# Attention and a gated feed-forward layer on one core: the last pair of token blocks in 26 products of 2x4x4 pieces in place of 28

## The chip, the cores and the metric

The kernel runs on one core of one Trainium2 chip. The metric is device time in microseconds (us) for one execution. Five engines work side by side: TensorE (PE in the profile; its weight loads are PEld), VectorE (DVE), ScalarE (ACT), GpSimd (POOL) and SyncE (SP), which issues the transfers. Each engine takes its own instructions in order and meets the others only through semaphores.

## The reference, cut to what matters

```python
scores = where(masks, q @ k.T / sqrt(64), -1e9)          # 8 batches x 8 heads, 576 x 576
attn   = softmax(scores) @ v
x      = attn.transpose(0, 2, 1, 3).reshape(4608, 512)
gate   = 1 / (1 + exp(-(x @ w_gate)))                     # w_gate, w_val: 512 x 1536
out    = (gate * (x @ w_val)) @ w_out                     # w_out: 1536 x 512
```

Heads 0 to 3 see a local window of 32 keys, heads 4 to 7 see keys at the same position modulo 32. All data is float32.

## The kernel before, in words

The tokens are cut into 9 blocks of 512. Blocks 0, 1 and 2 are multiplied plainly. The other six are taken two at a time: the constant `SUPER = (3, 5, 7)` names the first block of each pair, and the attention of later batches runs between the products of earlier blocks. Every float32 product is made of three TensorE instructions of 128 x 512: the high half of the weights times the high half of x, high times low, low times high. Each high half is a cast on ScalarE, each low half a subtraction (whole minus high) on VectorE or GpSimd.

For a pair k, gates and values are computed for two slices of 128 output features at a time (index q, six of them). One such unit multiplies two token blocks by two halves of the 512 input features by two feature slices, and Strassen's way takes 7 products in place of 8 (steps G for gates and V for values, `half_product`, L986). Each product covers two chunks of 128 input features, so it has 2 x 3 = 6 TensorE instructions: 7 x 6 x 2 x 6 = 504 for a pair. Results are summed in two PSUM banks for the gate and two for the value (tiles p and d). ScalarE copies some banks out (`keep_sum`, step c, L1008), VectorE adds the others to those copies (`add_sum`, step ad, L1013), ScalarE takes the sigmoid (sg) and VectorE multiplies gate and value (`gate_times`, step mu, L1030 and L1027). The 30 products of gate and value stay in SBUF as tiles `hid`.

The output of a pair is made in 7 products again (steps O, Oa, Ob, `out_half`, L1065, 252 TensorE instructions). Their operands are differences of `hid` tiles (`out_sum`, steps ta to td, L1036), split into a high half on ScalarE (hx, L1050) and a low half (hy on VectorE, hyp on GpSimd, L1054). There is room for five such operands at a time. While the output of one pair runs, the x operands of the next pair are made: differences of raw x (`diff`, xd on GpSimd, xdv on VectorE, L960), high halves (xh, L968) and low halves (xl, xlp, L972).

The weights in their sums and halves lie in DRAM (`sets`, `osets`) and come back through a ring of six places of 512 KB (`load_group`, steps r, L938 and L942), issued by SP.

The order of all this is one long list of step names, `ORDER`, written by a planner outside the program. The program walks the list once; each engine gets its instructions in the order of the list.

Of the kernel before, what the change touches and what calls it, by code (L numbers as in the profile page):

```python
# [22 lines left out]
P = 128  # L23
# [47 lines left out]

BANKS = {
# [18 lines left out]
fN0.3 wlp2.0 fg0.0.0 fP0.2 fX0.2 fW0.3 wb0.1 wa0.1 fg1.0.0 fH0.2 ws0.1 wr3.0 wb1.1 fT0.3 fL0.2 wa1.1 wd0.1 fR0.2 wr3.2 ws1.1 fg0.0.1 fP0.3 wd1.1 fS1.0
wu0.1 wu1.1 wl0.1 wb0.2 wlp1.1 fg1.0.1 fM1.0 fQ1.1 wa0.2 fg0.1.0 fA1.0 wr4.0 fg0.0.2 wa2.1 fU1.0 fg0.1.1 wb2.1 ws2.1 fX0.3 fE1.0 fY1.0 wr4.2 ws0.2
wdp2.1 wb1.2 fn1.0 fg1.1.0 fH0.3 fN1.0 wu2.1 fg0.1.2 fL0.3 fWp1.0 wa1.2 fg1.1.1 fR0.3 ws1.2 wr5.0 fg1.0.2 wlp2.1 fB1.0.1 fg0.0.3 fg0.1.3 fB1.0.0 s0.0
wdp0.2 fg1.0.3 wb2.2 m0.0 wa2.2 fg1.1.2 wdp1.2 fB1.0.2 x0.0 wr5.1 fg2.0.0 s0.1 fg2.1.0 y0.0 wu0.2 fg2.0.1 wu1.2 fB1.0.3 wa3.0 fg2.0.2 wb3.0 wb3.2
wl0.2 fg1.1.3 wl1.2 wa3.2 wa4.1 fg2.1.1 fg2.1.2 wa3.1 fg2.0.3 ws2.2 m0.1 fX1.0 wdp2.2 ws3.0 fZ1.1 fS1.1 ws4.1 ws3.2 ws3.1 wd3.0 fH1.0 fR1.0 fL1.0
fg2.1.3 wb3.1 wr6.0 wa4.0 x0.1 wu3.0 wdp3.1 wu3.1 wb4.0 wr6.2 y0.1 s0.2 m0.2 x0.2 wu2.2 wr5.2 ws4.0 wd4.0 wu4.0 wl4.0 wb5.0 o0.0 wdp3.2 o0.1 wu3.2
# [131 lines left out]
def attention_then_glu(ctx, tc, qk_l, qk_s, v_l, v_s, w_all, consts, out, out_t):  # L228
# [433 lines left out]
    def bank(tag, name):  # L662
        return (ps_a if tag == "a" else ps).tile([P, 2 * BANK], F32, tag=tag, name=name)
# [260 lines left out]
    for k in SUPER:  # L924
        units += [(k, q, p) for q in range(PAIRS) for p in USE] + [(k, p, u) for p in USE_OUT for u in range(PAIRS // 2)]
# [305 lines left out]
```

## Time and profile before

| What | Value |
|---|---|
| Three runs | 899.38, 900.62 and 901.22 us; median 900.62 us |
| Profiled execution, first to last instruction | 897.2 us |
| TensorE busy | 889.0 us, 99% of the span, 7050 matmuls |
| VectorE, ScalarE, GpSimd busy | 628.8, 477.8 and 327.8 us |
| Transfers | 193.63 MB, 216 GB/s over the span |
| Granted TensorE clock | 1.000 of full speed |

The profiled execution has no time of its own but its span of 897.2 us, which begins at the first and ends at the last instruction; the median of the three runs is 3.4 us above it, for what lies around the instructions and from run to run. A busy share is the time in which an engine has an instruction under way, waits inside an instruction included.

### The profile page before, as it was taken

To read this page: it belongs to the slowest core of one execution; us is meant where nothing else is said; L and a number is where in the kernel's file an instruction comes from. 1 tells how busy PE (TensorE), PEld (TensorE's weight loads), DVE (VectorE), ACT (ScalarE), POOL (GpSimd) and SP (SyncE) were. 2 spreads that over 40 slices of the span, in tenths; PEclk is the share of its full clock that TensorE was granted. 3 is DMA by queue.
4 is the path that set the end of the run, shared out by engine and by line. 5 is a ranking of instruction groups with operands and counts; after the bars stand their busy time and mean duration, and the time that the engine had idled before them with its cause. 6 is when DMAs were issued, how large, how long until landed. Compare 5 with 4: busy or idle time off the path is not lost.

```text
span 897.2 us, 17941 instructions
## 1 busy us (share of the span) xinstructions
PE 889.0 (99%) x7050; PEld 726.1 (81%) x7050; DVE 628.8 (70%) x1025; ACT 477.8 (53%) x869; POOL 327.8 (37%) x392
## 2 busy tenths in 40 slices
PE   8999999999999999999999999999999999999998
PEld 5788888888887788888878888888888888888886
DVE  6888877677778887889998976556667723433553
ACT  5888765443445554576564654344455623423453
POOL 4452631434663544675633420100132300221362
PEclk9999999999999999999999999999999999999999
DMA  9864685553573667898878758666655667655664
GB/s 349 331 229 138 217 280 168 165 163 109 158 247 99 178 182 267 245 323 288 252 249 274 258 181 271 219 205 198 216 180 194 214 192 232 195 176 204 235 205 148
DMA packets 116869, 193.63 MB, mean 216 GB/s; under 512 B 7600, under 2 KB 58800, under 8 KB 116784
## 3 DMA queue, kind: packets, MB, share of 16 engines
q1 hardware_dynamic: 116784, 192.47, 65.3%
q8 instruction: 56, 0.92, 0.4%
q14 instruction: 29, 0.24, 0.1%
HBM read 149.98 MB, written 42.47 MB: 214 GB/s over the span
## 4 chain that ended last, share of the span: by engine, by line
PE 89%; DVE 7%; ACT 2%; DMA 1%; issue 1%; SPq 0%; DVEq 0%; ACTq 0%
PE p L986 21%; PE oc L1065 19%; PE d L986 15%; PE o L713 10%; PE g L682 9%; PE v L682 9%; PE s L425 1%; PE x L603 1%; DVE pt L537 1%; PE gv L682 1%; PE x L575 1%; PE s_g L425 1%; DMA qk<-in_qk_l 1%; DVE sb L474 1%; ACT sb L489 1%
## 5 line engine op out<-in xcount | busy, mean ns | idle before, releaser
L986 PE MATMUL p<-xs,ring 128*128 128x512 f32 x864 | 210.9, 391 | 0.1
L986 PEld LDWEIGHTS p<-xs,ring 128*128 128x128 f32 x864 | 161.3, 188 | 34.2 <-issue 0.5
L986 PE MATMUL d<-xs,ring 128*128 128x512 f32 x648 | 160.0, 390 | 0.2 <-DVE hid L1013 0.2
L986 PEld LDWEIGHTS d<-xs,ring 128*128 128x128 f32 x648 | 121.2, 188 | 26.4 <-DVE hid L1013 0.9
L1065 PE MATMUL oc<-hh,ring 128*128 128x512 f32 x312 | 103.8, 389 | 0.0
L713 PE MATMUL o<-w,hh 128*128 128x512 f32 x288 | 90.5, 395 | 0.0
L1013 DVE TENSOR_TENSOR e<-e,d 128x512 f32<-128x512 f32 x54 | 37.0, 684 | 72.6 <-PE d L986 55.6
L682 PE MATMUL g<-xh,w 128*128 128x512 f32 x256 | 85.8, 393 | 0.8 <-DVE sb L449 0.5
L682 PE MATMUL v<-xh,w 128*128 128x512 f32 x256 | 85.0, 390 | 0.0
L1036 POOL TENSOR_TENSOR hid<-hid,hid 128x512 f32<-128x512 f32 x23 | 31.0, 1351 | 113.5 <-DVE hid L1030 87.8
L1065 PE MATMUL oc<-ops,ring 128*128 128x512 f32 x288 | 72.3, 389 | 0.0
L1050 ACT CAST hh<-hid 128x512 fp32r<-128x512 f32 x78 | 46.7, 620 | 42.9 <-PE oc L1065 31.5
L1065 PEld LDWEIGHTS oc<-hh,ring 128*128 128x128 f32 x312 | 58.6, 188 | 12.2
L1008 ACT COPY e<-p 128x512 f32<-128x512 f32 x54 | 31.7, 587 | 66.9 <-PE p L986 57.1
L1013 DVE TENSOR_TENSOR hid<-hid,d 128x512 f32<-128x512 f32 x54 | 36.8, 681 | 39.5 <-PE d L986 21.9
L898 POOL TENSOR_TENSOR sum<-w 128x256 f32<-128x256 f32 x49 | 39.4, 823 | 67.3 <-DMA sets<-sum 43.6
L1065 PEld LDWEIGHTS oc<-ops,ring 128*128 128x128 f32 x288 | 54.0, 188 | 11.3
L713 PEld LDWEIGHTS o<-w,hh 128*128 128x128 f32 x288 | 53.0, 188 | 11.4
L1008 ACT COPY hid<-p 128x512 f32<-128x512 f32 x54 | 31.7, 588 | 54.5 <-PE p L986 54.3
L1065 PE MATMUL oc<-hl,ring 128*128 128x512 f32 x156 | 60.7, 389 | 0.0
L903 POOL TENSOR_TENSOR sum<-sum 128x128 f32<-128x128 f32 x100 | 53.3, 534 | 18.8 <-DVE sum L898 5.5
L537 DVE STREAM_TRANSPOSE pt<-sb 32x320 f32<-32x320 f32 (+1 forms) x112 | 55.4, 495 | 3.3 <-POOL pt L376 1.0
(178 smaller groups left out, 1717.8 us busy)
## 6 DMA issues: line engine op xcount, KB each, us to landing
ring<-sets SPq DMA_DIRECT2D x126, 512.0 KB, 4.9
ring<-osets SPq DMA_DIRECT2D x63, 512.0 KB, 4.5
raw<-in_w_all SPq DMA_DIRECT2D x36, 512.0 KB, 5.7
qk<-in_qk_l SPq DMA_DIRECT2D x14, 608.0 KB, 5.0
qk<-in_qk_s SPq DMA_DIRECT2D x14, 594.0 KB, 5.4
sets<-w SPq DMA_DIRECT2D x24, 256.0 KB, 4.6
sets<-sumh SPq DMA_DIRECT2D x24, 256.0 KB, 2.9
sets<-sum SPq DMA_DIRECT2D x24, 256.0 KB, 3.1
```

The costliest lines, as they stand in the source:

```text
L425: nc.tensor.matmul(sc[j % len(sc)][g * m : (g + 1) * m, j // len(sc) * BANK + (s - lo) * kk : j // len(sc) * BANK + (s - lo + 1) * kk], q[ ...
L537: nc.vector.transpose(dst[band * LB : (band + 1) * LB, at : at + n, col * LB : (col + 1) * LB], src[part * LB : (part + 1) * LB, x : x + n ...
L682: nc.tensor.matmul(o, w, x, start=first and n == 0, stop=last and n == len(todo) - 1)
L713: nc.tensor.matmul(acc[k][i], h[:, i * P : (i + 1) * P], w, start=f == 0 and n == 0, stop=f == NF - 1 and n == 2,)
L898: by.tensor_tensor(to, part(wh[f][i], c), part(wl[f][i], c), op=ALU.add)
L903: by.tensor_tensor(u[:, to], u[:, x], u[:, y], op=op)
L986: nc.tensor.matmul(to, w[:, (wi * 2 + c) * P : (wi * 2 + c + 1) * P], x[xi][:, c], start=p in (1, 2, 5) and c == j == 0, stop=c == 1 and j ...
L1008: nc.scalar.copy(x, two[m, 0])
L1013: nc.vector.tensor_tensor(x, x, two[m, 1], op=ALU.add)
L1036: by.tensor_tensor(h[to], h[x], h[y], op=ALU.subtract)
L1050: nc.scalar.copy(ops[q, p][0], hidden_tile(k, q, KEPT[str(p)]))
L1065: nc.tensor.matmul(chains[m, at], w[:, (wi * 2 + m) * P : (wi * 2 + m + 1) * P], x[xi], start=p in (1, 2, 5) and q == j == 0, stop=q == PA ...
```

## The change

The gates and values of the last pair (blocks 7 and 8) are multiplied in another way. The unit is now two token blocks by four chunks of input features by four feature slices (index n, three of them, in place of six q). A scheme of 26 products replaces four times 7 = 28. Each product covers one chunk of 128 input features and so has 3 TensorE instructions: 26 x 3 x 2 x 3 = 468 for the pair in place of 504. The output of the pair is computed as before.

- The weight side has 24 sums per unit for the gate and 24 for the value (`W_SUMS`, 33 steps bu for each of the six combinations of n and gate or value, 128 x 128 each, 32 on GpSimd and one on ScalarE), then six high halves (bh, ScalarE) and six low halves (bw, VectorE), stored to DRAM by 14 transfers (bd) into `quad`, where four products lie side by side in rows of 2 KB. Two more slices are stored raw by `plain_sets`. The words that the sums start from are stored in DRAM while the earlier pairs' sets are made (wq, 24 transfers of 256 KB) and read back (bl, 6 transfers of 1 MB).
- The x side has 18 sums (`X_SUMS`, 12 on GpSimd as xq, 6 on VectorE as xqv), 24 high halves (xu, ScalarE) and 24 low halves (12 xw on VectorE, 12 xwp on GpSimd), in places listed in `SPOTS` and `X_AT`.
- The PSUM banks: the eight banks are eight tiles, four for the gate (m = 0) and four for the value (m = 1). A product p adds into the bank `CHAIN[p]`; running sums are read between products. `TAKEN` lists the 26 reads per gate or value: 8 copies on ScalarE (c) and 18 sums on VectorE (+, -, r). A bank is used again four products of the same kind later, with four of the other kind between. Gates end in tiles `ga`, then sigmoid (gs) and product (gm, 24 in all).
- The planner wrote the whole of `ORDER` anew. TensorE's own order is the same as before up to the first product of the last pair.

```diff
+PRODUCTS = 26
+CHAIN = (0, 1, 2, 3, 0, 1, 2, 3, 0, 1, 2, 3, 0, 1, 2, 3, 0, 1, 2, 3, 0, 1, 2, 3, 2, 3)
+CHAIN_STARTS = (0, 1, 2, 3, 18, 19)
+TAKEN = """
+0c1 1c5 2c6 3c0 4+5 5+1 6+0 6c3 7+6 7c7 8-7 9+3 12+3 13-7 14+1 15-5 16c2 17c4 18-0 19-6 20-6 21+0 22r2 23+4 24r3 25-7
+"""
...
+        if k == LAST:
+            units += [(k, "quad", n) for n in range(QUADS * PRODUCTS // 2)]
+        else:
+            units += [(k, q, p) for q in range(PAIRS) for p in USE]
...
+    def x_sum(n, by=nc.gpsimd):
+        to, a, b, op = x_sums[n]
+        by.tensor_tensor(x_word(to), x_word(a), x_word(b), op=ALU.add if op == "+" else ALU.subtract)
...
+    def x_low(n, by=nc.vector):
+        by.tensor_tensor(x_spot(X_AT[n][1]), x_word(f"x{n}"), x_spot(X_AT[n][0]).bitcast(F32), op=ALU.subtract)
...
+    def store_quad(n, m, u):
+        w = quad[n, m]
+        for part, x in ((0, word_high_at(w, u).bitcast(F32)), (1, w[u])):
+            for p, at, size in ((4 * u, 0, 4),) if u < 5 else ((20, 0, 2), (24, 2, 2)):
+                to = place_of(m, p)
+                nc.sync.dma_start(quad_set(n)[:, to // 4, part, to % 4 : to % 4 + size], x[:, at : at + size])
...
+    def quad_product(n, m, p):
+        at = place_of(m, p)
+        w = ring[LAST, "quad", n * (PRODUCTS // 2) + at // 4][:, :, at % 4]
+        x = X_OF[p]
+        high, low = (x_spot(n) for n in X_AT[x][:2])
+        for j, (wi, xi) in enumerate(((0, high), (0, low), (1, high))):
+            nc.tensor.matmul(
+                quad_bank(m, CHAIN[p]), w[:, wi], xi, start=p in CHAIN_STARTS and j == 0, stop=j == 2, skip_group_check=True
+            )
...
+    def take(n, m, j):
+        p, o, op = taken[j]
+        x, to = quad_bank(m, CHAIN[p]), part_of(n, m, o)
+        if op == "c":
+            nc.scalar.copy(to, x)
+        elif op == "r":
+            nc.vector.tensor_tensor(to, x, to, op=ALU.subtract)
+        else:
+            nc.vector.tensor_tensor(to, to, x, op=ALU.add if op == "+" else ALU.subtract)
```

What the new list does to the engines is seen in two places. The first is GpSimd while the output of the pair 5 is multiplied and just behind it. Before, the end of that stretch is this; `hl` and `ops` are low halves of output operands, `xs` low halves of x for the pair 7, `hid` sums for outputs. The last three rows already belong to the products of the pair 7.

```order
L1054 TENSOR_TENSOR ops_7207<-hid_9_7266,ops_7207 128x512
L1054 TENSOR_TENSOR ops_7207<-hid_11_7402,ops_7207 128x512
L1054 TENSOR_TENSOR hl_1_4_8090<-hid_3_6835,hh_1_4_8089 128x512
L1036 TENSOR_TENSOR hid_8_7222<-hid_8_7222,hid_7_7170 128x512
L1054 TENSOR_TENSOR ops_7207<-hid_8_7222,ops_7207 128x512
L1054 TENSOR_TENSOR hl_5_4_8125<-hid_13_7584,hh_5_4_8124 128x512
L972 TENSOR_TENSOR xs_3_1_7702<-xraw_7669,xs_3_0_7675 128x512
L1036 TENSOR_TENSOR hid_4_8395<-hid_3_8369,hid_2_8303 128x512
L1054 TENSOR_TENSOR hl_1_1_8425<-hid_2_8303,hh_1_1_8424 128x512
L1036 TENSOR_TENSOR hid_2_8303<-hid_4_8395 128x512
```

Now the same place reads as follows; L1163 is a sum of x pieces, L1169 a low half of x for the pair 7, L1292 a low half of an output operand of the pair 5.

```order
L1163 TENSOR_TENSOR xs_9_8340<-xraw_7845,xs_7_8004 128x512
L1163 TENSOR_TENSOR xs_12_8045<-xraw_7845,xs_10_8016 128x512
L1163 TENSOR_TENSOR xs_h_8348<-xraw_7845,xs_12_8045 128x512
L1163 TENSOR_TENSOR xs_9_8340<-xraw_7163,xs_7_8004 128x512
L1292 TENSOR_TENSOR ops_7974<-hid_9_7492,ops_7974 128x512
L1169 TENSOR_TENSOR xs_3_8111<-xs_7_8004,xs_2_8326 128x512
L1292 TENSOR_TENSOR ops_7974<-hid_11_7680,ops_7974 128x512
L1292 TENSOR_TENSOR hl_1_4_8420<-hid_3_7000,hh_1_4_8419 128x512
L1292 TENSOR_TENSOR ops_7974<-hid_8_7442,ops_7974 128x512
L1169 TENSOR_TENSOR xs_1_8188<-xs_6_7965,xs_0_7919 128x512
L1292 TENSOR_TENSOR hl_5_4_8481<-hid_13_7897,hh_5_4_8480 128x512
L1169 TENSOR_TENSOR xs_5_8400<-xs_8_8184,xs_4_8209 128x512
```

The same output operands are there, and between them now stand sums and low halves of x, most of which VectorE made before or which are new. From the first to the last TensorE instruction of this output, the list gives GpSimd 27 instructions of 128 x 512 (14 before), and VectorE 48 whose two inputs both lie in SBUF (55 before) and 8 that read a PSUM bank (6 before).

The second place is VectorE among the products of the last pair. Before, a stretch of it reads as follows; the rows with a tile `d` or `p` read a PSUM bank, the others multiply gate and value.

```order
L1013 TENSOR_TENSOR e_3_1_8580<-e_3_1_8580,d_3_8571 128x512
L1013 TENSOR_TENSOR hid_7_8588<-hid_7_8588,d_3_8615 128x512
L1030 TENSOR_TENSOR hid_7_8588<-hid_7_8588,e_3_1_8580 128x512
L1013 TENSOR_TENSOR hid_9_8656<-hid_9_8656,d_3_8615 128x512
L1013 TENSOR_TENSOR e_3_7_8646<-e_3_7_8646,d_3_8571 128x512
```

Now such a stretch, in the second of the three groups, is this; `q_2`, `q_3`, `qa`, `qg` and `qv` are PSUM banks, `qu` and `qw` weight sums (L1207 is a low half of them), L1268 multiplies gate and value.

```order
L1260 TENSOR_TENSOR ga_6_8900<-ga_6_8900,qg 128x512
L1207 TENSOR_TENSOR qu_0_8880<-qu_0_8880,qw_1_8878 128x512
L1258 TENSOR_TENSOR ga_2_9070<-q_2_8507,ga_2_9070 128x512
L1207 TENSOR_TENSOR qu_2_8884<-qu_2_8884,qw_1_8878 128x512
L1260 TENSOR_TENSOR hid_8_8973<-hid_8_8973,qv 128x512
L1260 TENSOR_TENSOR ga_4_9077<-ga_4_9077,q_3_8508 128x512
L1258 TENSOR_TENSOR hid_7_9093<-q_2_8511,hid_7_9093 128x512
L1260 TENSOR_TENSOR hid_6_8939<-hid_6_8939,q_3_8512 128x512
L1207 TENSOR_TENSOR qu_1_8887<-qu_1_8887,qw_1_8878 128x512
L1260 TENSOR_TENSOR ga_0_8928<-ga_0_8928,qa_8506 128x512
```

Low halves of the weights for the third group stand among the reads of the banks that the second group's products fill. From the first product of the last pair to the first of its output, the list gives VectorE 150 instructions: 107 that read a bank and 43 with both inputs in SBUF. Before they were some 61, 42 of them reads of a bank.

## Rows read from the trace of the kernel before

**Rows 1.** The page: busy time, and the granted clock in 40 slices.

```profile
PE 889.0 (99%) x7050; PEld 726.1 (81%) x7050; DVE 628.8 (70%) x1025; ACT 477.8 (53%) x869; POOL 327.8 (37%) x392
...
PEclk9999999999999999999999999999999999999999
```

**Rows 2.** Stretches: start:end, length, busy us (instructions) per engine, clock, DMA share, GB/s.

```profile
543.50:664.95 121.45, 121.45 (x850) 100.17 (x850) 70.50 (x114) 58.94 (x108) 16.23 (x19) 1.00 0.65 211
664.95:722.07 57.12, 57.12 (x253) 47.31 (x253) 42.18 (x62) 31.95 (x57) 18.29 (x13) 1.00 0.62 206
722.07:836.31 114.24, 114.24 (x505) 94.62 (x505) 40.53 (x60) 37.73 (x66) 16.31 (x13) 1.00 0.61 201
836.31:893.46 57.15, 57.14 (x252) 46.92 (x251) 30.32 (x38) 25.86 (x45) 28.98 (x22) 1.00 0.57 194
893.46:897.20 3.74, 0.00 (x0) 0.00 (x0) 0.00 (x0) 0.59 (x1) 0.00 (x0) 1.00 0.37 140
```

**Rows 3.** The chain that ended last, in order of time: start us, us, what.

```profile
664.95 57.12 PE oc L1065 x252
...
836.31 57.15 PE oc L1065 x252
```

**Rows 4.** Waits of VectorE from 722 to 840 us: total us, times, longest.

```profile
DVE e L1013 <- PE d L986: 32.8, 13, 7.5
```

**Rows 5.** Timeline of VectorE, 664 to 700 us: start us, us, instruction.

```profile
670.24 1.69 DVE L1036 TENSOR_TENSOR hid<-hid 128x512 f32<-128x512 f32 x1
671.84 0.68 DVE L960 TENSOR_TENSOR xd<-xraw,xd 128x512 f32<-128x512 f32 x1
672.45 0.68 DVE L1054 TENSOR_TENSOR hl<-hid,hh 128x512 fp32r<-128x512 f32 x1
673.05 0.68 DVE L1036 TENSOR_TENSOR hid<-hid 128x512 f32<-128x512 f32 x1
```

**Rows 6.** Timeline of GpSimd, 664 to 723 us.

```profile
670.08 1.29 POOL L1054 TENSOR_TENSOR hl<-hid,hh 128x512 fp32r<-128x512 f32 x1 [2.46 <-ACT hh L1050]
```

**Rows 7.** Timeline of GpSimd, 493 to 512 us.

```profile
495.54 1.75 POOL L960 TENSOR_TENSOR xd<-xraw,xd 128x512 f32<-128x512 f32 x1
497.25 1.73 POOL L1036 TENSOR_TENSOR hid<-hid 128x512 f32<-128x512 f32 x1
```

**Rows 8.** Timeline of VectorE in the same stretch.

```profile
496.49 1.35 DVE L1054 TENSOR_TENSOR hl<-hid,hh 128x512 fp32r<-128x512 f32 x1 [0.35 <-ACT hh L1050]
497.76 1.77 DVE L1054 TENSOR_TENSOR ops<-hid,ops 128x512 fp32r<-128x512 f32 x1
```

**Rows 9.** Groups of instructions from 500 us on: xcount, busy us, mean ns, idle before.

```profile
L1013 DVE TENSOR_TENSOR e<-e,d 128x512 f32<-128x512 f32 x36 | 24.7, 687 | 67.0 <-PE d L986 52.6 <-ACT e L1008 14.3
L1008 ACT COPY hid<-p 128x512 f32<-128x512 f32 x36 | 21.2, 588 | 47.8 <-PE p L986 47.7
```

**Rows 10.** GpSimd's sums of 128 x 128, whole execution, the same columns.

```profile
L903 POOL TENSOR_TENSOR sum<-sum 128x128 f32<-128x128 f32 x100 | 53.3, 534 | 18.8 <-DVE sum L898 5.5 <-ACT hid L1008 3.4 <-issue 2.9
```

**Rows 11.** Transfers from 722 to 836 us: total, and issues with median us to landing.

```profile
DMA packets 11377, 22.93 MB, mean 201 GB/s; under 512 B 721, under 2 KB 721, under 8 KB 11371
...
ring<-sets SPq DMA_DIRECT2D x38, 512.0 KB, 4.6
```

More of the change, by code (lines that the diff above doesn't have):

```diff
@@ L91 @@
[L91 to L94, printed above, removed]
@@ L876, in plain_sets @@
                 nc.sync.dma_start(sets[q][:, 7 * i + 2, n], b[:, 1])
+            for p in W_RAW:
+                k, f = divmod(W_RAW[p], 4)
+                if f // 2 == q % 2:
+                    for n, w in ((0, wh), (1, wl)):
+                        raw = w[2 * q + f % 2][i].bitcast(F32)[:, k * P : (k + 1) * P]
+                        to = place_of(i, p)
+                        nc.sync.dma_start(quad_set(q // 2)[:, to // 4, n, to % 4], raw)
     out_sets = {}
@@ L924, in attention_then_glu @@
     for k in SUPER:
[L925 removed]
+        if k == LAST:
+            units += [(k, "quad", n) for n in range(QUADS * PRODUCTS // 2)]
+        else:
+            units += [(k, q, p) for q in range(PAIRS) for p in USE]
+        units += [(k, p, u) for p in USE_OUT for u in range(PAIRS // 2)]
     groups, ring = [], {}
@@ new lines, in x_spot, with x_word @@
+    def x_spot(n, kind=F32R):
+        if (n, kind) not in x_spots:
+            t, at, many = x_tile(n, kind)
+            for j in range(many):
+                x_spots[at + j, kind] = t[:, j]
+        return x_spots[n, kind]
+    def x_word(name):
+        n = int(name[1:])
+        if name[0] == "x":
+            if n not in X_RAW:
+                return x_spot(X_AT[n][2], F32)
+            n = X_RAW[n]
+        return x_raw[LAST + n // NC][:, n % NC]
+    def x_sum(n, by=nc.gpsimd):
+        to, a, b, op = x_sums[n]
+        by.tensor_tensor(x_word(to), x_word(a), x_word(b), op=ALU.add if op == "+" else ALU.subtract)
@@ new lines, in attention_then_glu, with quad_bank @@
+    taken = []
+    for text in TAKEN.split():
+        op = next(o for o in "cr+-" if o in text)
+        taken.append((*(int(v) for v in text.split(op)), op))
+    def quad_bank(m, b):
+        if not quad_x:
+            both_banks.close()
+            ps_q = ctx.enter_context(tc.tile_pool(name="ps_q", bufs=1, space=bass.MemoryType.PSUM, side="right"))
+            for i, tag in ((0, "g"), (1, "v")):
+                quad_x[i, 0] = one_bank(tag, f"q{tag}")
+                quad_x[i, 1] = one_bank(f"a{i}", f"qa{i}")
+                for n in (2, 3):
+                    quad_x[i, n] = ps_q.tile([P, BANK], F32, tag=f"q{i}{n}", name=f"q{i}_{n}")
+        return quad_x[m, b]
@@ new lines, in quad_product, with part_of @@
+    def quad_product(n, m, p):
[7 more added lines that the diff above has]
+            )
+    gates = {}
+    def part_of(n, m, o):
+        j, f = divmod(o, 4)
+        if m:
+            return hidden_tile(LAST, 2 * n + f // 2, f % 2 + 2 * j)
+        if (n, o) not in gates:
+            gates[n, o] = work.tile([P, TB], F32, tag=GATE_TAGS[GATE_AT[n][o]], name=f"ga{n}_{o}")
+        return gates[n, o]
```

397 lines of the change are left out of this document (265 added, 132 removed).

## The prediction

> **What bounds the kernel now.** I read the page first: TensorE is busy for 889.0 of 897.2 us, at full granted clock in every slice [rows 1], which is the 2.4 GHz level. Busy time can hide waits inside pipelined instructions, so I went on to the stretches. The output of the pair 5 runs from 664.95 to 722.07 us, the gates and values of the pair 7 to 836.31, its output to 893.46, and in all three TensorE is busy for the whole stretch [rows 2]. The chain of what ended last says it more strictly: 252 output instructions in 57.15 us [rows 3], 226.8 ns each, with no gap between them; and 504 instructions in 114.24 us [rows 2], 226.7 ns each. So nothing but TensorE sets the end in the last 230 us, and an instruction taken from it there is worth its pitch of 0.2267 us, as long as the other engines still keep up. They do with ease while the pair 7 is multiplied: VectorE is busy for 40.5 of 114.2 us [rows 2], and its largest wait is for TensorE, up to 7.5 us at a time [rows 4].
>
> **The products.** 504 - 468 = 36 instructions go: 36 x 0.2267 = **-8.16 us**. TensorE's order before the last pair is unchanged, and the output behind it keeps its 252 instructions.
>
> **The output of the pair 5, where the x of the pair 7 is made.** This is the term that I expect to give part of it back. VectorE alone issues 128 x 512 instructions every 0.602 us (671.84, 672.45, 673.05, though each lasts 0.68) [rows 5]. But one that reads two SBUF tiles cannot run beside GpSimd: the one that started at 670.24 took 1.69 us, and ended 0.56 us after GpSimd's instruction of 670.08 to 671.37 [rows 5, 6]. The reverse is true as well: with both engines at work GpSimd's instructions last 1.73 to 1.75 us, each begun as the one before ends, and VectorE's stand between them, 1.35 and 1.77 us long [rows 7, 8]. A pair of one and one thus takes 1.74 us, and GpSimd's part of it is 1.74 - 0.60 = 1.14 us. Instructions that read a PSUM bank are outside of this: `e<-e,d` has a mean of 687 ns beside everything [rows 9].
>
> So I add, for this stretch, all VectorE instructions with two SBUF inputs and all of GpSimd's, counted from the two lists. Before: 55 x 0.602 + 14 x 1.14 = 33.1 + 16.0 = 49.1 us of work for one common way in 57.1 us, 0.86 of it, and TensorE did not wait. Changed: 48 x 0.602 + 27 x 1.14 = 28.9 + 30.8 = 59.7 us. That is 2.6 us more than the stretch has, if the way is never free, and both queues must reach their ends there: the last low halves of the output stand behind the x sums in GpSimd's row, as the first place of the order shows. If the way is used no better than before, at 0.86, the stretch needs 69.4 us, 12.3 more. I take 0.97, because two queues that are both behind leave little of it free (from 495.54 to 498.98 us two of GpSimd's and the VectorE instruction between them follow without a gap [rows 7, 8]), and because part of the work can start before the stretch: 59.7 / 0.97 = 61.5, **+4.4 us**, with 0 and 12.3 as ends. Zero is the low end and not 2.6, because GpSimd, busy for only 16.23 of the 121.45 us before [rows 2], may have run ahead.
>
> The Trainium skill, page "SBUF — State Buffer", section "Who interferes with whom", states that VectorE with two SBUF inputs and a GpSimd instruction that reads SBUF exclude each other for the whole instruction. Taken by whole durations (0.68 and 1.29 us) it would make 48 x 0.68 + 27 x 1.29 = 67.5 us, an estimate, and the stretch 10.4 us longer; the rows show overlapping ends, so the pitch decides.
>
> **Among the products.** VectorE gets 150 instructions in 468 x 0.2267 = 106.1 us, 107 of them reads of banks: 150 x 0.602 = 90.3 us, 85%. The other 43 meet GpSimd, which has 18 instructions of 128 x 512 and 64 sums of 128 x 128 there, 18 x 1.14 + 64 x 0.534 [rows 10] = 54.7 us, about half of the time. If half of the 43 wait for half of such an instruction (0.27 to 0.57 us), that is 6 to 12 us, at most 0.96 of the stretch. A bank must be read before the product that uses it again, seven products of 0.68 us later, 4.8 us, so single delays are covered. In the third group 58 VectorE instructions stand in 35.4 us, 35.0 us of pitch; there a delay is not made up at once, though the first output products do not need the last reads. I take **+1.2 us**, with 0 and 5 as ends. The copies and sigmoids on ScalarE cost nothing: it was busy for 37.7 of 114.2 us [rows 2], and 12 more copies at 0.588 [rows 9] and the casts fit into what is left.
>
> **Transfers, and the earlier stretches.** While the pair 7 is multiplied, 22.93 MB were moved at a share of 0.61 [rows 2, 11]. Changed: three ring loads of 0.52 MB fewer, two reads of 1 MB, 24 stores' worth of 6.3 MB: 29.7 MB in 106.1 us, 280 GB/s, which is 0.85 by the same ratio. While the pair 5 is multiplied it was 211 GB/s at 0.65 [rows 2], and some 11.5 MB are added in 121.45 us: 306 GB/s, 0.94. A ring load lands 4.6 us after its issue [rows 11], and the ring holds six units of 2.7 us, so a load can be 11 us late. I take 0. GpSimd's 192 sums of 128 x 128 lie mostly in stretches where it was idle (16.23 of 121.45 us [rows 2]); the same reason. What is behind the last output instruction, 3.74 us [rows 2], stays.
>
> **Sum.** -8.16 + 4.4 + 1.2 = -2.6 us. The profiled execution goes from 897.2 to 894.6 us of span; the median of the runs is 3.4 us above the span, 900.62, and goes to **898.0 us**.
>
> **Rivals.** *All is hidden.* GpSimd and VectorE work ahead, and the five operand places (five times 1.36 us of TensorE) bridge the crowded moments: -8.16 + 0 to 1 gives 892.5 to 893.5 us. For it: before, TensorE did not wait with the way used at 0.86, and where the output of the pair 7 ran GpSimd was busy for 28.98 and VectorE for 30.32 of 57.15 us, without a wait [rows 2]. Against it: 59.7 does not go into 57.1 unless work moves ahead, and the x sums wait for raw x of the last batch. Chance 0.24.
>
> *The common way costs more than the products give.* Slower than before is reached when the stretch of the pair 5's output grows by more than 8.16 + 1.8 - 1.2, some 9 us, that is, when the way is used at less than 59.7 / 66 = 0.90 of the time. VectorE's queue is strict: a low half that waits for ScalarE's cast holds up the sums behind it, GpSimd's chain of sums holds up VectorE's, and the way is free meanwhile. At 0.86 the time is 900.6 - 8.2 + 12.3 + 1.2 = 906 us; at 0.88, 904. For it: 0.86 is the only share that the trace shows for a whole such stretch. Against it: at 0.86 the queues were not behind, so it is no ceiling. The rule of the Trainium skill quoted above speaks for this one. Chance 0.22.
>
> *The transfers do not keep up.* At 0.94 of what 211 GB/s at 0.65 stands for, loads and stores of 512 KB queue; a store that waits for a late low half on VectorE holds every ring load behind it on SP. When a load is more than 11 us late, TensorE waits; 3 to 6 us would leave 898 less what it costs, 901 to 904 us with the other terms, 897 without them. Chance 0.12, half of it within 0.2% of now.
>
> My forecast, part of the gain given back before the last pair, has 0.42; its own range is 895.5 to 900.5 us.
>
> **How the numbers follow.** A measurement of this kernel can tell some 0.2%, 1.8 us (the three runs lie 1.84 us apart): faster means under 898.8, slower above 902.4. Faster: all of the 0.24, two thirds of my 0.42 (0.28): 0.52. Within 0.2%: the rest of mine 0.14, half of the transfers' 0.06, and the edge of the common way 0.04: 0.24. Slower: 0.24 in all. The range takes in the hidden case, with 0.3 us below it for the scatter of one median, and the slower one up to a share of 0.88: 892.2 to 904.0 us.
>
> **What would show it.** The pair's products take 106 to 108 us from first to last. The 252 output instructions of the pair 5 take 60 to 64 us in place of 57.12, with TensorE waiting for low halves of VectorE and GpSimd, and VectorE's instructions with two SBUF inputs have means well above 0.69 us there. If that stretch stays at 57.1, the second case is right; if it takes more than 66, the third. If ring loads land after more than 10 us and TensorE waits for them, the transfers. The prediction fails altogether if the earlier stretches, whose lists on VectorE, ScalarE, GpSimd and SP are all new, have waits of their own: nothing in my sum speaks of them.

## The result, and the profile after

The changed kernel takes 906.54 us (median of 20 executions, 902.14 to 910.32), the kernel before 900.77 us (20 executions, 897.89 to 904.07). The ratio is 1.0065, interval 1.0051 to 1.0079: slower by some 5.9 us, where 898.0 was forecast and 892.2 to 904.0 was the range. TensorE's clock is not what makes the difference: the executions with a mean granted clock of 1.000 have a median of 905.04 us with the changed kernel (7 of the 20) and of 899.31 us with the kernel before (37 of the 75 that were timed beside the experiments).

TensorE is still what is busy, and it has the 36 instructions fewer. The line of the page on it:

```profile
PE 887.7 (98%) x7014; PEld 720.1 (79%) x7014; DVE 723.9 (80%) x1134; ACT 502.2 (55%) x928; POOL 464.4 (51%) x603
```

TensorE's instructions come in the same order up to the pair 7, so the stretches can be set side by side. First the changed kernel, in the columns of [rows 2]: the plain part, products and output of the pair 3, of the pair 5, of the pair 7.

```profile
0.00:360.24 360.24, 352.21 (x3591) 283.73 (x3592) 281.13 (x488) 207.24 (x387) 161.10 (x217) 1.00 0.70 228
360.24:494.63 134.39, 130.90 (x1229) 106.36 (x1229) 115.91 (x192) 79.55 (x147) 88.05 (x128) 0.99 0.85 275
494.63:553.78 59.15, 59.15 (x381) 48.60 (x382) 55.60 (x78) 35.78 (x67) 20.29 (x16) 1.00 0.71 248
553.78:677.55 123.77, 122.10 (x849) 99.99 (x850) 85.16 (x132) 65.25 (x122) 67.02 (x116) 1.00 0.87 299
677.55:738.39 60.84, 59.13 (x254) 46.90 (x253) 55.63 (x59) 32.35 (x60) 39.66 (x27) 1.00 0.63 213
738.39:846.02 107.63, 107.06 (x470) 87.53 (x469) 95.56 (x144) 52.54 (x97) 55.41 (x82) 1.00 0.83 285
846.02:903.14 57.12, 57.12 (x252) 46.95 (x251) 34.89 (x46) 28.87 (x49) 32.84 (x23) 1.00 0.53 176
```

The first three stretches of the kernel before, which the prediction did not look at:

```profile
0.00:355.09 355.09, 350.93 (x3591) 283.60 (x3592) 279.48 (x487) 210.71 (x391) 160.51 (x217) 1.00 0.63 204
355.09:484.39 129.30, 129.00 (x1230) 104.92 (x1229) 114.36 (x193) 78.88 (x142) 70.39 (x97) 1.00 0.83 270
484.39:543.54 59.15, 59.15 (x381) 48.60 (x382) 51.51 (x74) 33.20 (x61) 17.08 (x13) 1.00 0.71 239
```

The other four stand in [rows 2]. From the output of the pair 5 on, things went nearly as forecast: 60.84 us in place of 57.12, then 107.63 in place of 114.24, then the same 57.12. The loss is ahead of that: +5.15 in the plain part, +5.09 and +2.3 in the products of the pairs 3 and 5, 12.6 us in all between these two traces. In the four stretches ahead TensorE has nothing under way for 13.2 us, before for 4.5.

The two traces lie further apart than the kernels do. The changed kernel's is of an execution of 908.58 us, 2.0 above its median, and the kernel before took 4.7 us more ahead of the output of the pair 5 when it was traced again (e12 below); between the two second traces the loss ahead is 7.0 us. By the medians it is some 8.7 us: the 5.8 us of difference, and the 2.9 us that the stretches behind gain. TensorE's longest waits in three windows of the first trace (120 to 131, 440 to 480, 655 to 690 us; total, times, longest):

```profile
PE x L656 <- DMA vv<-in_v_s: 2.4, 1, 2.4
...
PE p L1075 <- issue: 2.0, 1, 2.0
PE p L1075 <- DVE hid L1116: 1.4, 1, 1.4
...
PE p L1075 <- ACT e L1097: 1.2, 1, 1.2
PE oc L1303 <- DMA ring<-osets: 0.5, 1, 0.5
PE oc L1303 <- DVE hl L1292: 0.4, 1, 0.4
```

Each is a wait for something else: a load, nothing that the trace names ("issue"), VectorE, ScalarE, an output weight load. No single resource is full.

### The profile page after: what moved, and what is told of

It reads as the page before. It is cut to its first block, busy times and chain, and to the rows that moved or that the text cites. A ratio compares the mean times of both kernels' runs of the same rounds, so it can differ in the third digit from the quotient of the medians.

```text
span 906.8 us, 18603 instructions
## 1 busy us (share of the span) xinstructions
PE 887.7 (98%) x7014; PEld 720.1 (79%) x7014; DVE 723.9 (80%) x1134; ACT 502.2 (55%) x928; POOL 464.4 (51%) x603
## 4 chain that ended last, share of the span: by engine, by line
PE 80%; DVE 7%; ACT 4%; DMA 4%; issue 2%; POOL 1%; SPq 1%; DVEq 0%; ACTq 0%; POOLq 0%
PE oc L1303 18%; PE p L1075 12%; PE d L1075 10%; PE g L735 9%; PE v L735 8%; PE o L766 7%; PE q L1238 6%; PE qa L1238 2%; PE qv L1238 1%; PE qg L1238 1%; PE s L478 1%; PE x L656 1%; DVE pt L590 1%; DMA quad<-qw 1%; DMA sets<-w 1%
## 5 line engine op out<-in xcount | busy, mean ns | idle before, releaser
L1075 PE MATMUL p<-xs,ring 128*128 128x512 f32 x576 | 141.8, 392 | 4.6 <-issue 2.0
L1075 PEld LDWEIGHTS p<-xs,ring 128*128 128x128 f32 x576 | 107.0, 188 | 28.4 <-issue 2.4
L1075 PE MATMUL d<-xs,ring 128*128 128x512 f32 x432 | 108.4, 395 | 0.1
L1075 PEld LDWEIGHTS d<-xs,ring 128*128 128x128 f32 x432 | 81.9, 190 | 18.2 <-DVE hid L1102 0.5
L983 POOL TENSOR_TENSOR sum<-sum 128x128 f32<-128x128 f32 x100 | 55.6, 558 | 47.3 <-DMA quadw<-sum 32.1
L1195 POOL TENSOR_TENSOR qu<-qw 128x128 f32<-128x128 f32 x96 | 48.7, 525 | 58.9 <-DMA qw<-quadw 45.7
L1292 DVE TENSOR_TENSOR hl<-hid,hh 128x512 fp32r<-128x512 f32 x55 | 51.9, 962 | 16.8 <-ACT hh L1288 15.2
L735 PEld LDWEIGHTS v<-xh,w 128*128 128x128 f32 x256 | 48.0, 188 | 11.8 <-DVE sb L497 1.0
L735 PEld LDWEIGHTS g<-xh,w 128*128 128x128 f32 x256 | 48.0, 188 | 10.7 <-ACT e L743 0.5
L766 PE MATMUL o<-w,hl 128*128 128x512 f32 x144 | 56.1, 390 | 0.0
```

The lines of the kernel that those rows point to most:

```text
L735: nc.tensor.matmul(o, w, x, start=first and n == 0, stop=last and n == len(todo) - 1)
L766: nc.tensor.matmul(acc[k][i], h[:, i * P : (i + 1) * P], w, start=f == 0 and n == 0, stop=f == NF - 1 and n == 2,)
L983: by.tensor_tensor(u[:, to], u[:, x], u[:, y], op=op)
L1075: nc.tensor.matmul(to, w[:, (wi * 2 + c) * P : (wi * 2 + c + 1) * P], x[xi][:, c], start=p in (1, 2, 5) and c == j == 0, stop=c == 1 and j ...
L1195: by.tensor_tensor(to, a, word_slot(w, b), op=ALU.add if op == "+" else ALU.subtract)
L1292: by.tensor_tensor(hl, hidden_tile(k, q, KEPT[str(p)]), hh.bitcast(F32), op=ALU.subtract)
```

## The experiments

Each kernel was timed in alternation with the kernel before on the same chip; what is compared is the ratio to that. The stretches are from one profiled execution each (us):

| Kernel | Ratio, interval | Plain | Products 3 | Products 5 | Output 5 | Products 7 |
|---|---|---|---|---|---|---|
| before | 1 | 355.1 | 129.3 | 121.4 | 57.1 | 114.2 |
| changed | 1.0065, 1.0051 to 1.0079 | 360.2 | 134.4 | 123.8 | 60.8 | 107.6 |
| e1_no_prep | 1.0040, 1.0022 to 1.0057 | 360.1 | 131.9 | 122.5 | 59.8 | 107.4 |
| e2_no_transfers | 1.0057, 1.0039 to 1.0075 | 357.0 | 133.2 | 123.4 | 59.9 | 107.6 |
| e3_no_work | 1.0040, 1.0018 to 1.0062 | 361.0 | 131.6 | 122.5 | 60.9 | 107.4 |
| e4_xsums_vector | 1.0115, 1.0089 to 1.0141 | 358.8 | 134.3 | 123.8 | 63.8 | 107.2 |
| e5_two_loads_later | 1.0067, 1.0044 to 1.0090 | 360.6 | 130.9 | 124.9 | 61.0 | 107.6 |
| e6_old_plain_order | 1.0573, 1.0548 to 1.0599 | 404.6 | 134.3 | 123.7 | 60.3 | 107.9 |
| e7_both | 1.0558, 1.0535 to 1.0582 | 404.2 | 132.3 | 123.5 | 60.1 | 107.7 |
| e8_fewer_products | 0.9911, 0.9891 to 0.9930 | 354.8 | 129.8 | 121.4 | 57.1 | 106.3 |
| e9_operands_early | 1.0001, 0.9985 to 1.0017 | 357.5 | 134.2 | 122.0 | 59.1 | 107.4 |
| e10_x_on_gpsimd | 1.0150, 1.0118 to 1.0183 | 363.8 | 137.5 | 123.8 | 63.7 | 108.4 |
| e11_after_again | one execution | 360.1 | 133.2 | 124.1 | 60.7 | 107.4 |
| e12_before_again | one execution | 358.4 | 130.7 | 121.4 | 57.1 | 114.2 |
| e13_five_moves | 1.0135, 1.0108 to 1.0161 | 359.7 | 136.7 | 125.4 | 61.6 | 107.6 |
| e14_three_moves | 1.0107, 1.0073 to 1.0140 | 361.0 | 134.1 | 125.2 | 61.6 | 107.6 |
| e15_two_moves | 1.0063, 1.0042 to 1.0083 | 356.8 | 132.5 | 125.1 | 60.3 | 107.6 |

The two outputs that the table leaves out took 59.1 to 59.6 us (pair 3) and 57.1 (pair 7) in every trace.

**What is chance.** Two traces of the same kernel came first for judging the table.

> The changed kernel once more, for a second trace. What belongs to the program comes again within 0.5 us: the stop without a releaser in the pair 3's products (2.3 us), the wait of 1.8 us for VectorE 25 us later, the output of the pair 5 at 60.8 us. What does not come again (the wait of 2.4 us for V at 128 us, shifts in the first 30 us) is chance of the transfers.

> The kernel before once more, for a second trace: from 33 us on the stretches within 0.5 us of the first trace (129.3, 59.2, 121.4, 57.1, 114.2, 57.1 us); if its executions differ by 6 us, the difference lies in the first 30 us and in the plain part.

The changed kernel repeats within 1.2 us in every stretch, and its stops come again at the same instructions: V (the load of attention's values, `vv`) 2.2 us, "issue" 2.1, VectorE 1.4, ScalarE 1.2, in place of 2.4, 2.0, 1.4 and 1.2. V was put down to chance wrongly: in all seven traces with this part of the order and its stores TensorE waits for it, though between 0.3 and 2.4 us. The kernel before repeats within 0.1 us from the output of the pair 3 on, not within 0.5 in the two stretches ahead. Its plain part is 3.3 us longer, all of it ahead of 33 us, and the reason is TensorE's clock, here from 20 to 28 us in the second trace and then in the first:

```profile
20.00:28.00 8.00, 8.00 (x135) 6.39 (x131) 5.01 (x11) 5.25 (x16) 3.57 (x3) 0.53 1.03 409
```

```profile
20.00:28.00 8.00, 7.47 (x212) 5.56 (x208) 6.71 (x14) 6.91 (x16) 3.05 (x3) 1.00 1.03 409
```

At 0.53, which is the level of 1.2 GHz nearly all the time, 135 matmuls are done where 212 were. The traces of e1, e3, e6, e7, e10 and e13 have 1 to 4 us of the same kind there, so up to 4 us of the plain column are chance. Over whole executions it is the same: the 14 of the 75 whose mean granted clock was under 0.9955 have a median of 903.2 us, against the 899.3 at 1.000. The products of the pair 3 differ by 1.4 us between the two traces of before: there too TensorE stopped once for no named reason ("issue", 1.2 us at 448 us).

**Is it the new work, or the new order?** Three kernels take away the weight side as a whole, its transfers alone, its instructions alone.

```diff
-    names = ORDER.split()
+    names = [w for w in ORDER.split() if w.rstrip("0123456789.") not in ("wq", "bl", "bu", "bh", "bw", "bd")]
```

That is e1 (without the raw stores too; the products then read `sets`). e2 leaves out wq, bd and the raw stores, e3 bu, bh and bw.

> The changed kernel without any of its added weight-side work: no sums, high and low halves of weight sums, no stores of them, no store and reload of the words, no raw stores; the products of the last pair read the weight sets of the earlier pairs instead, by as many loads of 512 KB, so the output is not the reference's. The new order of all other steps, and the x side, stay. Theory A (the weight side, in whatever way, costs the 12.6 us that the changed kernel lost before the output of the pair 5): the stretches up to the end of the pair 5's products come back to within 2 us of the kernel before, the output of the pair 5 stays 2 to 4 us long through the x sums, in all 889 to 893 us. Theory B (the planner's new order of the old steps costs it): at least 6 of the 12.6 us stay, 897 us or more.

> The weight sums, high and low halves are computed as in the changed kernel, but nothing of them is stored: no word stores, no set stores, no raw stores; the six reads of 1 MB read the earlier sets, the products too, so the output is not the reference's. Some 27 MB and 132 transfers fewer, all instructions of the engines kept. Theory C (transfers cost the early 12.6 us: SP's queue, late loads, waits for a store to land before a tile is used again): at most 4 us of the 12.6 stay, 891 to 896 us. Theory D (the added instructions on VectorE, ScalarE and GpSimd delay what TensorE waits for): at least 8 us stay, 901 us or more.

> The reverse: all added transfers stay at their places and sizes, but the 198 weight sums, 36 casts and 36 low halves are not computed; the stores take words that were loaded, so the output is not the reference's. Theory C (transfers): at least 8 of the 12.6 us stay before the output of the pair 5, 900 to 906 us. Theory D (instructions): at most 4 stay, 891 to 896 us.

Theory A falls (889 to 893 us were expected by it). With no weight-side work at all the kernel is still slower than before, 1.0040; all of that work is worth 0.25% (2.2 us), by the two intervals at most about twice that. C and D, as sole causes, fall with it: without the transfers and without the instructions alike the kernel stays at 904 to 905 us. What they do show is small: by traces e2 (work kept) against e1, the instructions cost 1.3 and 0.9 us in the products of the pairs 3 and 5; by e3 against e1, the transfers cost 1.1 us in the output of the pair 5.

What the 36 products are worth in the old order:

```diff
             for j, (wi, xi) in enumerate(((0, 0), (0, 1), (1, 0))):
+                if k == SUPER[-1] and p in (2, 6, 7) and c == 0 and j == 1:
+                    continue
                 nc.tensor.matmul(
```

> The kernel before, in its own order, with 36 of the 504 TensorE instructions of the pair 7 left out (high times low in the first chunk of three of the seven products), so the output is not the reference's. What 36 instructions are worth alone: 36 x 0.2267 = 8.16 us less than the kernel before, 891.5 to 892.8 us, the pair's products 106.1 us, if TensorE alone sets the end there; over 894 us if another engine takes over.

As expected: 0.9911 of 899.86 us is 8.0 us less, and the pair's products run without a gap:

```profile
722.21:828.54 106.33, 106.33 (x469) 87.69 (x469) 40.02 (x60) 37.62 (x66) 16.64 (x13) 1.00 0.66 215
```

e1 and e8 both lack the 36 products and all weight-side work; e1 has the new order of everything and the new x side. Their ratios stand 1.0040 / 0.9911 = 1.013 apart, 11.6 us, give or take 2.4 us by the two intervals. Of these the output of the pair 5 (59.8 against 57.1) and the products of the pair 7 (107.4 against 106.3) are 3.8 us; the other 7.8 us lie in stretches where the two kernels compute nearly the same thing (VectorE has 116 instructions among the products of the pair 5, before 114). Some 1.5 us of them can be the clock, whose mean was 0.996 in the executions of e1 and 0.998 in those of e8. The rest, some 6 us, is put down to Theory B, the new order of old steps, because nothing else of size is left; e9 (below) shows a part of it directly.

**The old order put back.** The list of the kernel before up to `V3.0.1`, with each store of words (wq) between the sums pa and pb of the old list; one of the 24 places:

```diff
-pav0.1.1 s1.3 LQ2 wq0.1.1 m1.3 pb0.1.0 ph0.1.0.1 pw0.1.0 pd0.1.0 Y1 x1.3 B1.0 B1.1 pa1.0.0 y1.3 pbv0.1.1
+pav0.1.1 wq0.1.1 pbv0.1.1
```

> The changed kernel, same output, with the order of the kernel before up to the first product of the pair 3, into which only the 24 word stores are put, each behind the sum that it stores; from there on the new order. Theory B (the new order of old steps costs time): the plain part goes back from 360.2 to 355 to 356.5 us, in all 901 to 903 us. Rival (the added word stores and raw stores delay loads there, whatever the order): the plain part stays at 358 us or more, 904 us or more in all.

> Both of the two edits (the old order of the plain part, two ring loads later), same output. If both theories hold the gains add: 897 to 900 us, level with the kernel before or a little faster. If either falls: 901 us or more.

Both came out some 50 us above what Theory B said, so they do not decide about it: something else costs more here. A store of words reads the tile that the next sum (pb) overwrites, so that sum, and GpSimd's whole row behind it, waits until the store has landed. GpSimd's waits from 130 to 404 us of e6 (total, times, longest):

```profile
POOL sum L978 <- DMA sets<-sum: 58.0, 13, 10.5
POOL sum L983 <- DMA quadw<-sum: 43.5, 14, 7.5
```

In the changed kernel (130 to 360 us) they are

```profile
POOL sum L983 <- DMA quadw<-sum: 32.1, 11, 6.6
...
POOL sum L978 <- DMA sets<-sum: 18.8, 8, 6.2
```

One such wait of e6 can be followed to TensorE, in the timelines of GpSimd and ScalarE (start, us, instruction, idle time before it and what ended it):

```profile
168.30 2.05 POOL L983 TENSOR_TENSOR sum<-sum 128x128 f32<-128x128 f32 x4 [7.53 <-DMA quadw<-sum]
170.38 0.62 ACT L988 CAST sumh<-sum 128x512 fp32r<-128x512 f32 x1 [7.70 <-POOL sum L983]
172.31 0.60 ACT L743 ACTIVATE e<-g 128x512 f32<-128x512 f32 x1
```

The cast of the late sum stands ahead of a sigmoid in ScalarE's row, and TensorE waits for that sigmoid, 4.7 us. It does so five times from 130 to 404 us:

```profile
PE g L735 <- ACT e L743: 14.5, 5, 4.7
```

Behind the stops of this stretch the granted clock is 0.50 for 31 us in all, which is at most 15 of the 44 us that the plain part grew by.

So the old order with the stores at these places is far worse than the new one. Whether other places for them would do in the old order was not tried. e7 adds only that its second edit works here as in e5 (below): the pair 3's products take 132.3 us in place of 134.3.

**The stop without a releaser.** At 450.56 us TensorE stops for 2.0 us between the fourth and the fifth instruction of one product. Its windows (stretch, busy us per engine, clock, DMA share, GB/s):

```profile
443.00:450.00 7.00, 7.00 (x142) 5.61 (x142) 6.71 (x13) 5.72 (x11) 2.11 (x5) 1.00 0.96 328
...
453.00:456.00 3.00, 3.00 (x9) 2.31 (x8) 1.91 (x4) 2.14 (x5) 0.95 (x1) 0.54 0.33 125
```

The DMA engines were full for 7 us ahead of it, and behind it the clock falls to the level of 1.2 GHz for some 3 us. In the second trace it does not fall here, but behind the wait for V:

```profile
130.50:133.90 3.40, 3.40 (x9) 2.65 (x9) 2.31 (x6) 1.78 (x4) 0.00 (x0) 0.50 1.07 355
```

So a stop of about 2 us can cost nearly 2 us more (3.4 us at half the clock). The queue that carries instructions, from 450 to 452 us, after none of its packets from 430 to 450:

```profile
q1 hardware_dynamic: 741, 0.48, 75.9%
q8 instruction: 1, 0.02, 3.1%
```

Over the span this queue moves 55 packets, 0.90 MB; for 14,028 matmuls and weight loads that is 64 bytes each, so I take it for TensorE's code, 16 KB at a time. The packets of all 17 traces bear this out. In each of them the packet is the 35th of that queue, the place is the same one in TensorE's program (give or take one matmul), and TensorE goes on there 1.2 to 1.5 us after the packet has landed, however long it stood. Six of them (us; the third column counts the matmuls and weight loads that TensorE still had ahead of the place when the packet started):

| Trace | Packet starts | Instructions ahead of the place | Packet has landed | TensorE goes on | Stop |
|---|---|---|---|---|---|
| before | 442.50 | 91 | 443.43 | 444.88 | 0.1 |
| before, second trace | 446.96 | 8 | 447.93 | 449.35 | 1.2 |
| changed | 450.12 | 1 | 451.10 | 452.56 | 2.0 |
| changed, second trace | 450.60 | none | 451.57 | 452.83 | 2.1 |
| e10_x_on_gpsimd | 455.70 | none | 456.70 | 458.02 | 3.4 |
| e5_two_loads_later | 448.17 | 111 | 449.18 | 450.65 | 0.2 |

e5 makes the burst ahead of it smaller.

```diff
-LV16 ... r27 r25 R15 r26 X16.1 pwp4.2.0 pd4.2.0
+LV16 ... r27 R15 X16.1 pwp4.2.0 pd4.2.0 r25 r26
```

> The changed kernel, same output, with two ring loads of 512 KB (r25, r26) issued some 8 us later: behind the output weight store and ahead of the loads that follow it, no longer in the burst of 441.6 to 445.7 us. Theory E (TensorE's own code waits behind that backlog: at 450.6 us TensorE stops for 2.3 us inside a product with no releaser, its 16 KB of code starts only at 450.12 us, and its clock is low behind it): the stop goes, the pair 3's products take 130.5 to 131.5 us in place of 134.4, in all 3 to 4 us less, 901.5 to 903 us. Rival (the stop is a wait that the trace does not name, for VectorE or for the ring): it stays within 0.5 us, 904.5 to 907 us.

The stretch does what Theory E says, 134.4 to 130.9 us, and the stop is gone; DMA share and waits there:

```profile
443.00:450.00 7.00, 7.00 (x144) 5.68 (x143) 6.74 (x12) 6.38 (x12) 3.29 (x6) 1.00 0.76 249
```

```profile
PE p L1075 <- DMA ring<-sets: 1.6, 1, 1.6
```

In its place a ring load comes 1.6 us late, and the median does not fall at all (1.0067, though its interval leaves room for 2 us). All eleven traces of the new order in which this burst was left alone have the stop, 1.7 to 3.4 us long. That the late packet makes it is shown by the table, and that the burst makes the packet late by e5. A full set of DMA engines is not needed for it: the second trace of the kernel before stops here with a DMA share of 0.75 in the 7 us ahead.

**The output of the pair 5.** Its x sums are moved to VectorE, and in the next kernel x steps of VectorE to GpSimd:

```diff
-xq6 ... xq3 ... xq0 ... xq7 ... xq10 ... xq1 xq13 ... xq9 ... xq4 xq12 ... xq15 ... xq16
+xqv6 ... xqv3 ... xqv0 ... xqv7 ... xqv10 ... xqv1 xqv13 ... xqv9 ... xqv4 xqv12 ... xqv15 ... xqv16
```

> The changed kernel with its 12 x sums of GpSimd moved to VectorE, at the same places in the order; same output. If the common way of VectorE and GpSimd makes the output of the pair 5 long, its work there falls by about 11 x (1.14 - 0.60) = 6 us, and the stretch from 60.8 to 57.1 to 58.5 us, in all 903 to 905 us. If the stretch is long because store landings hold ScalarE at its start, or because VectorE's own row is too full, it stays at 60 us or gets longer, 906 to 910 us.

```diff
-xqv5 ... xqv14 ... xqv8 ... xw3 ... xw1 ... xqv17 ... xqv11
+xq5 ... xq14 ... xq8 ... xwp3 ... xwp1 ... xq17 ... xq11
```

> The changed kernel, same output, with seven of its x steps in the output of the pair 5 (5 sums, 2 low halves) moved from VectorE to GpSimd, at the same places in the order. By the common way of the prediction that is 7 x (1.14 - 0.60) = 3.8 us more work for it: the stretch grows from 60.8 to 62 to 65 us, in all 907 to 911 us. If instead VectorE's own row is the limit there (it was busy for 55.6 of 60.8 us, and the reverse move cost 3 us), the stretch falls to 58 to 60 us, in all 903 to 906 us.

The stretch grew both ways, to 63.8 and 63.7 us (e4, then e10):

```profile
676.05:739.86 63.81, 59.67 (x254) 46.69 (x253) 53.93 (x69) 32.51 (x60) 24.27 (x17) 1.00 0.59 204
```

```profile
684.26:747.95 63.69, 59.31 (x253) 46.62 (x253) 52.91 (x50) 32.09 (x59) 49.87 (x33) 1.00 0.59 202
```

With more on GpSimd the stretch went as the sum over the common way says (62 to 65); the whole kernel took 914.9 us, above the 907 to 911 expected, at a mean granted clock of 0.991. With more on VectorE the sum says 6 us less work, and the stretch still took 3 us more. In e4 VectorE's low halves are as short as before the change, and TensorE waits longer for them (0.6 us in all in the changed kernel):

```profile
L1292 DVE TENSOR_TENSOR hl<-hid,hh 128x512 fp32r<-128x512 f32 x19 | 13.7, 747 | 3.8 <-ACT hh L1288 3.8
```

```profile
PE oc L1303 <- DVE hl L1292: 2.7, 4, 1.3
```

So the sum alone is not a model of the stretch. What I think limits it besides is VectorE's row, in which low halves of operands and x sums stand in turn and each waits for the one ahead; no run takes that apart from the rest.

**The operands' places.** The weight sums borrow the tiles in which the first five operands of an output are made (tags hh0 to hl2). Before, the casts `hx5.0.1` to `hx5.4.1` stood 76 to 19 of TensorE's product steps ahead of the output; in the changed list 7 to none. e9 is e1 with these operands as early as in the old list: 20 steps move, the casts and low halves of the first five operands of the pairs 3 and 5, and nothing else. For the pair 5:

```diff
-hx5.0.1 hy5.0.1 c5.5.0.6 ... hx5.1.1 hy5.1.1 ... hx5.2.1 tc5.0 ... hx5.3.1 ... hy5.3.1 ... Oa5.0.1 hy5.2.1 ... hx5.4.1 hy5.4.1
+hx5.0.1 ... hy5.0.1 ... hx5.1.1 ... hy5.1.1 hx5.2.1 ... hy5.2.1 hx5.3.1 hy5.3.1 ... hx5.4.1 ... hy5.4.1 ... Oa5.0.1
```

> The kernel without the weight-side work of e1_no_prep (output not the reference's), and with the first five operands of the outputs of the pairs 3 and 5 made as far ahead as in the kernel before; with the weight sums in their places, the changed kernel makes them only in the last microseconds before the output. Theory F (the borrowed operand places cost the stop of 0.7 to 1.5 us just before the output of the pair 5 and the waits in its first 8 us): the pair 5's products take 121.4 us as before (e1: 122.5), its output 58 to 59 us (e1: 59.8), the pair 3's products 130 to 131 us; in all 2 to 3 us less than e1, 901 to 902.5 us. Rival (the end of that output, with the x sums in the rows of VectorE and GpSimd, is what counts): within 1 us of e1, 903 to 905 us.

900.34 us, ratio 1.0001: 3.5 us less than e1 (the intervals do not meet; some 1 us can be the clock), and from 655 to 690 us TensorE waits for nothing. So the new places of these old steps did cost time. By its traces the two stretches that the theory names give 1.2 us of it (182.3 to 181.1); the pair 3's products did not gain (134.2, with the stop at 449 us). The rest is not located, and the plain part, 2.6 us shorter, is mostly chance of the clock.

**Can the stops be moved away?**

```diff
-pl1 ... LV0
+LV0 pl1
-ad3.3.1.7 LQ18 ... r27 r25 R15 r26
+ad3.3.1.7 r27 r25 LQ18 ... R15 r26
-V5.5.6 xu15 ... hx5.0.1 hy5.0.1 c5.5.0.6 G5.5.7 c5.5.1.6
+V5.5.6 c5.5.0.6 c5.5.1.6 xu15 ... hx5.0.1 hy5.0.1 G5.5.7
-r88 bd1.1.4 ... r90 Oa5.0.1
+r88 r90 bd1.1.4 ... Oa5.0.1
-bw0.0.4 tav3.2 G3.4.3 ad3.4.0.3 r31 sg3.4.3 mu3.4.4
+G3.4.3 ad3.4.0.3 r31 sg3.4.3 mu3.4.4 bw0.0.4 tav3.2
```

> The changed kernel, same work and output, with five moves of steps in the order, one for each place where the two traces of the changed kernel agree that TensorE stops before the pair 7: (a) a set store of 12 transfers (pl1) goes behind the loads that it stood ahead of, so that V of 127 us comes in time; (b) two ring loads go ahead of a load of Q that waits for its place, so that the burst behind it is smaller and TensorE's code comes in time; (c) two copies of sums out of their banks go ahead of casts of x and weight sums on ScalarE (the wait of 1.5 us at 666 us); (d) an output weight load goes ahead of stores of weight sums in SP's queue (the wait of 0.8 to 1.5 us at 679 us); (e) a low half of weight sums and a difference on VectorE go behind the product of gate and value that TensorE's bank waits for (1.8 us at 475 us). If these causes are right: the plain part 357 to 358.5 us, the pair 3's products 129.5 to 131.5, the pair 5's products 122 to 123, the output of the pair 5 60 to 61, in all 897 to 900.5 us. Rival (the stops only move on, since the rows are full all the way): 902 to 906 us.

> The same with (c), (d) and (e) alone, the moves that take nothing from the transfers' chance: 2.5 to 4 us less than the changed kernel, 902 to 903.5 us, with the late V at 127 us and the stop without a releaser at 450 us still there. If the gains of (c) to (e) are taken up by later waits: 904.5 us or more.

> The changed kernel, same work and output, with only the moves (a) and (e) of e13: the set store of 12 transfers behind the loads that it stood ahead of, and the low half and the difference on VectorE behind the product that TensorE's bank waits for. In e13 the stops at 127 and 475 us were gone. If these two are losses of their own, the plain part is 357 to 358 us, no stop of over 1 us comes at 475 us, and the kernel takes 2 to 4 us less than the changed one, 902 to 904.5 us; if they come back at later places, 905 to 908 us.

None came out as hoped. e13 is slower than the changed kernel, 1.0135, and e14 too, 1.0107, though its interval (1.0073 to 1.0140) meets the changed kernel's. In e13 the stop for V and the one for VectorE at 475 us are gone, and the one without a releaser is down to 1.0 us, but (b) makes a load of Q late and (c) a sum on VectorE:

```profile
PE s L478 <- DMA qk<-in_qk_l: 3.9, 1, 3.9
...
PE d L1075 <- DVE e L1102: 2.0, 2, 1.5
```

e15, with (a) and (e) alone, has no wait for V in its trace and 0.2 us of wait for VectorE, but its stop without a releaser is 1.0 us longer:

```profile
PE p L1075 <- issue: 3.0, 1, 3.0
```

Its profiled execution is 4.2 us shorter than the changed kernel's, yet the median of its 12 executions is not (905.8 us, 1.0063), and at a mean granted clock of 1.000 the two are level: 904.9 us (5 executions) and 905.0 (7). The trace of the changed kernel was of one of its slower executions. So the two waits can be taken away, and no gain from it was measured. No version with the reference's output beat the kernel before.

## Why the prediction was wrong

The step that failed is the term for transfers and the earlier stretches, which was put at 0. The runs show some 8.7 us there by the medians, more than the products give.

- **The products** were right: 36 x 0.2267 = 8.16 us forecast, 8.0 measured by e8.
- **The output of the pair 5**: +4.4 forecast, +3.7 (3.5 in the second trace). VectorE's low halves `hl` have a mean of 1127 ns there, before 743, as the lock between two SBUF inputs and GpSimd makes them:

```profile
L1292 DVE TENSOR_TENSOR hl<-hid,hh 128x512 fp32r<-128x512 f32 x19 | 20.9, 1127 | 2.0 <-ACT hh L1288 2.0
```

 The Trainium skill, page "SBUF — State Buffer", section "Who interferes with whom", has that rule; counted with whole durations it asked for 67.5 us (the prediction's estimate), and the stretch took 60.84, so the pitch was the better price. So much of the mechanism is in the trace. But the term was meant for the x sums, and these alone cost 2.0 us (e9: 59.1 against 57.1); 0.7 more come from the late operands (e1 against e9) and 1.0 with the weight-side work (the changed kernel against e1). And e4 makes the low halves short again without making the stretch shorter, so the sum over the common way is not what sets its length. The size was more than twice too large for the x sums, and the total right by accident.
- **Among the products**: +1.2 forecast, 107.63 - 106.1 = +1.5; 107.4 without the weight sums (e1), so most of it is not theirs.
- **Transfers, and the earlier stretches**: the step that failed. "I take 0", since GpSimd was idle there and ring loads had room; it was +12.6 us between the first traces, 7.0 between the second, 8.7 by the medians. The rates themselves were near (306 GB/s at a share of 0.94 forecast for the products of the pair 5, 299 at 0.87 measured). I priced what is added by the idle share of engines, and left out that the planner had to set every old step anew to fit it in. Taking all weight-side work away gives back only 2.2 us (e1), so most of the loss is not the added work itself; some 6 of the 7.8 us between e1 and e8 are left for the new order, by exclusion. Of its mechanisms the runs show two: old steps that lost their lead (e9; that they lost it because their places are lent is my reading of the list), and a burst of loads that makes a packet of TensorE's code late (e5). A third, sums that wait for a store of the tile that they overwrite, belongs to the added stores; it is what made the old order so slow with them (e6).
- **The rivals.** "All is hidden" fell with the output of the pair 5, 60.8 us and not 57.1. "The common way costs more" gave 904 to 906 us, near the measured 906.5, but by a way that was not the one: the stretch took 60.8 us, not 66. "The transfers do not keep up" saw that loads can be late (V does come late), but placed it in ring loads of the pair 5, and its sign did not show: in the page ring loads land after a median of 4.5 to 5.6 us, and TensorE waits for one 0.5 us. Without all these transfers (e2) the kernel is as slow.
- The last line of the prediction named the gap, waits in the earlier stretches, and gave it no term and no share of the range.

Open: of what the new order's 6 us or so consist, place by place; e9 accounts for a part of them, and the old order itself could not be measured with the stores in it. The scatter of the executions, 8 us, hides gains of 1 to 2 us.

## What to carry to other kernels

When a change makes a planner write the whole order anew, the new order is a term of its own: compare the two lists ahead of the edit too, and look for steps that lost their lead (here the operands, whose tiles were lent). An engine's idle share does not say that work added to it is free: what counts is which tile the work borrows or holds until a store has landed, and what stands behind it in the row. And the gain itself is cheap to measure alone (e8): leave the instructions out of the old kernel first, then see how much room the preparation may cost. Where TensorE stops and the profile names no releaser ("issue"), look at the queue that carries instructions.

## What the runs showed of the hardware

- One place in TensorE's program waits for a 16 KB packet of the instruction queue: in all 17 traces TensorE goes on there 1.2 to 1.5 us after the packet has landed, whether it stood for 0.1 us (before) or for 3.4 us (e10). With the DMA engines at a share of 0.96 for 7 us the packet started when TensorE had all but reached the place, and the stop was 2.0 us; with two loads of 512 KB moved out and a share of 0.76 it started 111 instructions ahead, and the stop was 0.2 us (e5).
- Behind a stop of about 2 us the granted clock was 0.50 for 3.4 us in some traces and 1.00 in others, with the same program: in the first trace of the changed kernel behind the stop at 450 us, in the second behind the wait for V. From 20 to 28 us it was 0.53 or 1.00 from one execution of the kernel before to the next, and the plain part took 3.3 us more or less with it; a good part of the scatter of 6 to 8 us is the clock.
- A store of a 256 KB tile that the next sum overwrites holds that sum for 3 us on the mean (43.5 us in 14 waits of e6), 7.5 at the longest.
- In the output of the pair 5 VectorE's low halves, which read two SBUF tiles, took 743 ns on the mean while GpSimd worked for 18.3 us of the stretch, 747 ns with 24.3 us (e4), and 1127 ns with 39.7 us.
